# Experts 1 to 3 of a fused attention and expert kernel: word conversion dealt out 3, 1, 2, 2, weight splits begun one place sooner, two tiles for converted words

## The chip, the core and the metric

One core of a Trainium2 chip runs the whole program. The metric is the device time in microseconds of one execution; the time given for a kernel is the median of its runs. The engines are TensorE (PE in the rows; its weight loads PEld), VectorE (DVE), ScalarE (ACT), GpSimd (POOL) and SyncE (SP), which issues nearly all transfers from one in-order queue (SPq).

## The reference

Three layers follow one another: a gated linear recurrence over 768 positions, four experts mixed by normalised probabilities, and a feed-forward layer with h − tanh(h).

```python
# recurrence, for each of 4 x 8 heads of width 48
state = alpha[:, :, t, :, None] * state + np.einsum('bhd,bhe->bhde', k[:, :, t], v[:, :, t])
y[:, :, t] = np.einsum('bhd,bhde->bhe', q[:, :, t], state)
# four experts on x of 3072 x 384, w1[e] 384 x 1024, w2[e] 1024 x 384
for e in range(E):
    h = np.maximum(x @ w1[e], 0.0)
    out += p[:, e:e + 1] * (h @ w2[e])
# last layer, w_in 384 x 2048, w_out 2048 x 384, given in float64
h = x @ w_in
g = h - np.tanh(h)
return (g @ w_out).astype(np.float32)
```

The weights of the last layer are float64, so the chip gets them as 64-bit words and turns them into float32 itself.

## The kernel before

The program has three stages. In the first (about 0 to 332 us) the recurrence runs in chunks, woven into expert 0. In the second (about 332 to 921 us) experts 1, 2 and 3 run on all 3072 tokens. In the third (921 us to the end) the last layer runs. Every float32 product is made from three passes in a faster format: each operand is split into a high part (a cast on ScalarE, `hi`) and a low part (a subtraction on GpSimd, `lo`), and the product is high·high + low·high + high·low.

The change lies in the second stage and in the last block of expert 0 before it. The second stage is 36 **steps**, numbered 0 to 35 here: for each expert g = 1, 2, 3, three pairs of token blocks (p = 0, 1, 2, each block 512 tokens), and for each pair four pairs of feature tiles (fp = 0 to 3). A step is one call of `pair_stage`. It computes four 128x512 tiles of x @ w1 by a scheme that shares sums and differences of weights (`ws`, made by `w_pair`) and of tokens (`tb`, `ta`, made by `forms`), so that eleven products of three matmuls do the work of twelve. Each of the four results ends in one VectorE sum, in this order: L713 (`pc`), L727 (`u`), L736 (`pa`), L743 (`u2`). After each sum come the ReLU on ScalarE (`hh`, L596) and the low part on VectorE (`hl`, L597), and then the generator yields; I call the point after it a **place**, 0 to 3. After a place, `mm2` runs nine matmuls with w2 for a tile that was finished three places earlier.

At each place the caller also issues pieces of side work:

- `conv_all` (generator `bits`) converts the last layer's weights, in 32 pieces of 128x384 words. A piece takes six VectorE instructions, its **words**: L49, L52, L55, L58, L61, L65. Its result is then split by a ScalarE cast (L478) and a GpSimd subtraction (L479) into the tile `wo`, and SyncE stores `wo` to DRAM (`w64s`). There is one `wo` tile, so the cast for one piece waits for the store of the piece before.
- `w_pair` splits two weight tiles, in four pieces, one at each place: first `hi(wa)` on ScalarE with four short sums on GpSimd (L447 to L450, for `ws`); then `lo(wa)` and `hi(wb)`; then `lo(wb)` and `hi(ws)`; then `lo(ws)` and the loads of the next two raw weight tiles (`wraw`, two buffers).
- `forms` prepares the token sums in steps 1, 2, 5 and 6.

The Tile framework puts the semaphores in, and each engine runs its instructions in the order of the program. PSUM holds two tiles for the four results (`pa`, `pc`), so a product that reuses one of them waits for the sum that reads it: the last product of a step, made with s4 of `ws`, waits for L736.

Of the kernel before, what the change touches and what calls it, by code (L numbers as in the profile page):

```python
# [10 lines left out]
F32R = mybir.dt.float32r  # L11
# [30 lines left out]
def words_to_f32(nc, pool, raw, res):  # L42

    n = raw.shape[1]
    r2 = raw.bitcast(I32).rearrange("p (n two) -> p n two", two=2)
    lo, hi = r2[:, :, 0], r2[:, :, 1]
    t1 = pool.tile([P, n], I32, name="t1", tag="t1")
    t3 = pool.tile([P, n], I32, name="t3", tag="t3")
    nc.vector.tensor_scalar(out=t1, in0=hi, scalar1=3, scalar2=0x7FFFFFFF,  # L49
                            op0=ALU.logical_shift_left, op1=ALU.bitwise_and)  # L50
    yield
    nc.vector.scalar_tensor_tensor(out=t1, in0=hi, scalar=-2147483648, in1=t1,  # L52
                                   op0=ALU.bitwise_and, op1=ALU.bitwise_or)
    yield
    nc.vector.tensor_scalar(out=t3, in0=lo, scalar1=29, scalar2=0x40000000,  # L55
                            op0=ALU.logical_shift_right, op1=ALU.bitwise_or)
    yield
    nc.vector.tensor_tensor(out=t3, in0=t1, in1=t3, op=ALU.bitwise_xor)  # L58
    yield
    t5 = pool.tile([P, n], I32, name="t5", tag="t5")  # L60
    nc.vector.tensor_scalar(out=t5, in0=hi, scalar1=1, scalar2=21,  # L61
                            op0=ALU.logical_shift_left, op1=ALU.logical_shift_right)
    yield
    wf = pool.tile([P, n], F32, name="wf", tag="wf", bufs=2)
    nc.vector.scalar_tensor_tensor(out=wf, in0=t5, scalar=897.0, in1=f32(t3), op0=ALU.is_ge, op1=ALU.mult)  # L65
    res.append(wf)
# [117 lines left out]
def tile_kernel(ctx: ExitStack, tc: tile.TileContext, qka, a0, v, vT, pT, w12, w64, out):  # L184
# [281 lines left out]
    def conv_all(pool):  # L466

        raws, wfs, outs = [], [], []

        def load(i, half):  # L470
            raw = pool.tile([P, 384], I64, name="r64", tag="r64", bufs=2)
            nc.sync.dma_start(out=raw, in_=w64[i, :, half])
            raws.append(raw)

        def store(i, half):
            wf = wfs.pop(0)
            o = pool.tile([P, 2, 384], F32R, name="wo", tag="wo")
            nc.scalar.copy(o[:, 0], wf)  # L478
            nc.gpsimd.tensor_tensor(out=o[:, 1], in0=wf, in1=f32(o[:, 0]), op=ALU.subtract)  # L479
            outs.append((i, half, o))  # L480

        load(*conv[0])
        load(*conv[1])
        yield
        for k, (i, half) in enumerate(conv):
            for j, _ in enumerate(words_to_f32(nc, pool, raws.pop(0), wfs)):
                yield
                if j == 1 and k:
                    store(*conv[k - 1])
                    if k + 1 < len(conv):  # L490
                        load(*conv[k + 1])
                if j == 4 and outs:
                    i_, h_, o = outs.pop()
                    nc.sync.dma_start(out=w64s[i_][:, :, h_], in_=f32(o))
            yield
        store(*conv[-1])
        yield
        i_, h_, o = outs.pop()
        nc.sync.dma_start(out=w64s[i_][:, :, h_], in_=f32(o))
# [251 lines left out]
    with tc.manual_schedule():  # L751
# [106 lines left out]
        for si, st in enumerate(steps0):  # L858
            g, bi, t0, n, f, last = st
            bl = blocks0  # L860
            if f == 0:
                nxt = (g, *bl[bi + 1]) if not last else None
                if last:
                    early.close()
                    late["p"] = main.enter_context(tc.tile_pool(name="psx", bufs=1, space=PSUM))
                    late["w"] = main.enter_context(tc.tile_pool(name="wx", bufs=1))
                    acc.extend(late["w"].tile([P, KB, 512], F32, name=f"acc{i}", tag=f"acc{i}") for i in (4, 5))
                    late["s"] = mid.enter_context(tc.tile_pool(name="pairs", bufs=1))
                    late["c"] = mid.enter_context(tc.tile_pool(name="conv", bufs=1))
                    side = [forms(0, h, form_load(0, h)) for h in range(2)]  # L870

                if not last:
                    first, goal = done[0], ready((bl[bi + 1][0] + bl[bi + 1][1]) // C - 1) + LEAD
                    loaded = split = False
                    share = [first + (goal - first) * k // 16 for k in range(17)]
            ph = mm1(st)
            evac1(st, ph)
            pend.append(st)
            if not last:
                points(min(goal, share[2 * f + 1]))  # L880
            flush({5: 2, 6: 3, 7: 3}.get(f, 1) if last else 1)
            if not last:
                points(min(goal, share[2 * f + 2]))
                if not loaded and done[0] >= goal - LEAD:
                    loaded = True
                    x_load(*nxt)
                    p_load(*nxt)
                if not split and done[0] >= goal - LEAD + 3:
                    split = True
                    for kb in range(KB):  # L890
                        x_parts(*nxt[1:], kb)
                if bi == 0 and f < 4:
                    w_prep(4 + f)
                if bi == 0 and f == 4:
                    w_load(8)
                    w_load(9)
                    p_norm()
                    p_load(0, 0, 256)
            else:

                if f == 1:
                    pair_tile(0)
                    pair_tile(1)
                if f == 2:
                    for j in range(KB):
                        pair_load(0, j, 0)
                if f in (2, 6):
                    side.append(w_pair(8 + f // 4 * 2))
                if 1 <= f < 5:
                    for _ in range(2):  # L910
                        next(side[(f - 1) // 2], None)
                for t in side[2:]:
                    next(t, None)
                if f == 6:
                    for j in (0, 2, 1):
                        pair_load(1, j, 0)
                if f == 2:
                    fl = late["w"].tile([112, NU], F32, name="fl", tag="fl")
                    nc.vector.tensor_scalar(out=fl, in0=flags, scalar1=2.0 ** 60, scalar2=None, op0=ALU.is_le)
                    rs = late["w"].tile([112, 1], F32, name="rs", tag="rs")  # L920
                    nc.vector.tensor_reduce(out=rs, in_=fl, axis=mybir.AxisListType.X, op=ALU.add)
                if f == 3:
                    pc = rolling(0)[0:1, 0:1]
                    nc.tensor.matmul(pc, rs, ones, start=True, stop=True)
                    ci = const.tile([1, 1], I32, name="ci", tag="ci")
                    nc.vector.tensor_copy(ci, pc)
                if f == 5:
                    ok_count = nc.values_load(ci, min_val=0, max_val=112 * NU)
            if f == 3:
                x_keep(t0, n)  # L930
# [8 lines left out]
        for k, (g, p, fp) in enumerate(group):  # L939
            if k in (0, 4):  # L940
                raw = [form_load(k // 4 + 1, h) for h in range(2)]
            if k in (1, 2, 5, 6):
                side.append(forms(k // 4 + 1, k % 4 - 1, raw.pop(0)))

            if p == 2 and fp > 1:
                j = (g + 1) * 8 + 2 * fp - 4
            elif p == 0 and fp in (1, 2):
                j = g * 8 + 2 + 2 * fp
            else:
                j = None  # L950
            if j is not None and j < 32:
                side.append(w_pair(j))
            for pos in pair_stage(g, p, fp, fp == 3 and k + 1 < len(group)):
                po_out()
                if k > 2:
                    for _ in range(2 if fp and not (k in (5, 6) and pos < 2) else int(pos == 1)):
                        next(bits, None)
                for t in side:
                    next(t, None)
                if k == len(group) - 1 and pos >= 1:  # L960
                    x_split(4, 0, pos - 1)
            if fp == 1:
                for n in range(2):
                    p_load(g, (2 * p + n) * 512, 512)
            if j is not None and j >= 32:
                w_prep(j)
                w_prep(j + 1)
# [87 lines left out]
```

## Time and profile before

| | |
|---|---|
| median of 3 runs | 1334.12 us (1333.34 to 1334.77) |
| the profiled execution's own time | 1332.25 us |
| its span, first to last instruction | 1330.4 us |
| TensorE busy | 1287.2 us, 97% |
| VectorE busy | 896.9 us, 67% |
| ScalarE busy | 609.4 us, 46% |
| GpSimd busy | 536.0 us, 40% |
| mean granted TensorE clock | 0.989 |

Busy times of TensorE are made from pipelined matmuls whose ends are modelled, so 97% is not a share of its peak. What can be won without fewer matmuls is the time in which TensorE waits. The profiled execution is 1.87 us below the median of the runs.

### The profile page before, as it was taken

To read this page: it belongs to the slowest core of one execution; us is meant where nothing else is said; L and a number is where in the kernel's file an instruction comes from. 1 tells how busy PE (TensorE), PEld (TensorE's weight loads), DVE (VectorE), ACT (ScalarE), POOL (GpSimd) and SP (SyncE) were. 2 spreads that over 40 slices of the span, in tenths; PEclk is the share of its full clock that TensorE was granted. 3 is DMA by queue.
4 is the path that set the end of the run, shared out by engine and by line. 5 is a ranking of instruction groups with operands and counts; after the bars stand their busy time and mean duration, and the time that the engine had idled before them with its cause. 6 is when DMAs were issued, how large, how long until landed. Compare 5 with 4: busy or idle time off the path is not lost.

```text
span 1330.4 us, 18547 instructions
## 1 busy us (share of the span) xinstructions
PE 1287.2 (97%) x6747; PEld 1049.9 (79%) x6748; DVE 896.9 (67%) x1383; ACT 609.4 (46%) x1096; POOL 536.0 (40%) x487
## 2 busy tenths in 40 slices
PE   6799999999999999999999999999999999999997
PEld 4688888887878787778887788888888888888885
DVE  7678667624456657766666666665878787878785
ACT  3334333323433334333333333334777777777764
POOL 4211011004433134532044522114777676767664
PEclk8899999999999999999999999999999999999999
DMA  8365544416462725462616251517200000000000
GB/s 269 100 179 149 155 138 122 146 50 216 164 233 92 247 71 202 128 210 82 213 56 245 86 190 64 202 52 293 98 22 3 24 2 25 0 25 0 24 1 27
DMA packets 86389, 153.24 MB, mean 115 GB/s; under 512 B 7568, under 2 KB 43664, under 8 KB 86032
## 3 DMA queue, kind: packets, MB, share of 16 engines
q1 hardware_dynamic: 76304, 147.24, 33.1%
q10 hardware_dynamic: 9984, 4.72, 1.4%
q8 instruction: 55, 0.90, 0.3%
q14 instruction: 46, 0.38, 0.1%
HBM read 115.71 MB, written 36.23 MB: 114 GB/s over the span
## 4 chain that ended last, share of the span: by engine, by line
PE 83%; DVE 6%; DMA 3%; issue 3%; ACT 2%; POOL 2%; SPq 0%; POOLq 0%; DVEq 0%; ACTq 0%
PE po L641 39%; PE ph L589 21%; PE ph L674 18%; PE pa L308 2%; DMA w64s<-wo 2%; PE pa L341 1%; PE pa L344 1%; DVE hl L597 1%; ACT hh L596 1%; DMA wraw<-w 1%; POOL tb L547 1%; DVE fg L260 1%; PE ph L779 1%; PE pa L303 1%; PE pa L333 1%
## 5 line engine op out<-in xcount | busy, mean ns | idle before, releaser
L641 PE MATMUL po<-hh,w 128*128 128x512 f32 (+1 forms) x1776 | 451.1, 389 | 0.0
L641 PEld LDWEIGHTS po<-hh,w 128*128 128x128 f32 x1776 | 327.4, 189 | 74.0 <-issue 3.5
L589 PE MATMUL ph<-xt,w 128*128 128x512 f32 (+1 forms) x1368 | 326.7, 385 | 0.3 <-DVE ptmp L663 0.3
L589 PEld LDWEIGHTS ph<-xt,w 128*128 128x128 f32 x1368 | 251.8, 192 | 52.5 <-issue 1.2
L641 PE MATMUL po<-hl,w 128*128 128x512 f32 (+1 forms) x888 | 247.7, 387 | 1.2 <-DVE hl L621 1.2
L674 PE MATMUL ph<-xt,w 128*128 128x512 f32 x864 | 234.2, 392 | 1.7 <-DVE hl L597 0.9
L641 PEld LDWEIGHTS po<-hl,w 128*128 128x128 f32 x888 | 165.8, 190 | 35.9 <-DVE hl L621 1.6
L674 PEld LDWEIGHTS ph<-xt,w 128*128 128x128 f32 x864 | 162.3, 188 | 38.2 <-DVE hl L597 1.3
L596 ACT ACTIVATE hh<-ph 128x512 fp32r<-128x512 f32 (+1 forms) x128 | 73.1, 571 | 244.3 <-PE ph L589 145.0
L597 DVE SCALAR_TENSOR_TENSOR hl<-ph,hh 128x512 fp32r<-128x512 f32 (+1 forms) x128 | 84.1, 657 | 143.5 <-ACT hh L596 143.4
L75 POOL TENSOR_SCALAR gmk<-gu 128x512 int32<-128x512 f32 x96 | 143.1, 1491 | 49.0 <-ACT gu L71 48.3
L621 POOL TENSOR_TENSOR hl<-gg,hh 128x512 fp32r<-128x512 f32 x94 | 121.8, 1296 | 54.1 <-ACT hh L619 54.1
L479 POOL TENSOR_TENSOR wo<-wf,wo 128x384 fp32r<-128x384 f32 x32 | 35.1, 1098 | 235.4 <-ACT wo L478 235.4
L702 ACT COPY ut<-ph 128x512 f32<-128x512 f32 x108 | 63.3, 586 | 115.3 <-PE ph L674 115.3
L674 PE MATMUL ph<-xt,ws 128*128 128x512 f32 x324 | 106.6, 399 | 9.7 <-DVE ph L736 5.6
L71 ACT ACTIVATE gu<-ph 128x512 f32<-128x512 f32 x96 | 57.6, 600 | 114.7 <-PE ph L589 68.7
L667 POOL TENSOR_TENSOR acc<-acc,ptmp 128x512 f32<-128x512 f32 x51 | 65.0, 1295 | 102.3 <-DVE ptmp L663 102.3
L76 DVE SCALAR_TENSOR_TENSOR ghu<-ph,gu 128x512 f32<-128x512 f32 x96 | 66.3, 691 | 51.8 <-ACT gt L72 51.5
L674 PEld LDWEIGHTS ph<-xt,ws 128*128 128x128 f32 x324 | 60.8, 189 | 28.2 <-DVE ph L736 8.6
L80 DVE COPY_PREDICATED gg<-gmk,ph 128x512 f32<-128x512 int32 x96 | 72.0, 750 | 10.1 <-POOL gmk L75 0.3
L365 POOL TENSOR_TENSOR state<-state,fc 112x192 f32<-112x192 f32 x20 | 10.1, 506 | 169.9 <-DVE state L356 145.4
L79 DVE SCALAR_TENSOR_TENSOR gg<-gs,ghu 128x512 f32<-128x512 f32 x96 | 66.4, 692 | 14.9 <-DVE ghu L78 2.9
(121 smaller groups left out, 1512.3 us busy)
## 6 DMA issues: line engine op xcount, KB each, us to landing
xt<-xs SPq DMA_DIRECT2D x54, 512.0 KB, 5.8
xt<-xb SPq DMA_DIRECT2D x27, 512.0 KB, 5.7
r<-w SPq DMA_DIRECT2D x32, 384.0 KB, 5.0
w64s<-wo SPq DMA_DIRECT2D x32, 384.0 KB, 3.0
w<-w64s SPq DMA_DIRECT2D x16, 768.0 KB, 7.4
qk<-qka SPq DMA_DIRECT2D x24, 448.0 KB, 6.8
wraw<-w SPq DMA_DIRECT2D x26, 384.0 KB, 5.2
pb<-pn SPq DMA_DIRECT2D x23, 256.0 KB, 4.6
```

The costliest lines, as they stand in the source:

```text
L75: nc.gpsimd.tensor_scalar(out=mk, in0=u, scalar1=T2, scalar2=None, op0=ALU.is_gt)
L76: nc.vector.scalar_tensor_tensor(out=hu, in0=ph, scalar=C4, in1=u, op0=ALU.mult, op1=ALU.mult)
L79: nc.vector.scalar_tensor_tensor(out=gg, in0=s2, scalar=B2, in1=hu, op0=ALU.add, op1=ALU.mult)
L80: nc.vector.copy_predicated(out=gg, mask=mk, data=ph)
L589: nc.tensor.matmul(ph[:, :n], w[:, a, 0, kb * P:(kb + 1) * P], x[:, b, kb, :n], start=m == 0, stop=m == len(seq) - 1)
L596: nc.scalar.activation(a[:, :n], ph[:, :n], AF.Relu)
L597: nc.vector.scalar_tensor_tensor(out=b[:, :n], in0=ph[:, :n], scalar=0.0, in1=f32(a[:, :n]), op0=ALU.max, op1=ALU.subtract)
L621: eng.tensor_tensor(out=b, in0=gg, in1=f32(a), op=ALU.subtract)
L641: nc.tensor.matmul(po[d, pool][:, :n], w[:, wi, 1, d * P:(d + 1) * P], r[:, :n], start=first and pi == 0, stop=last_ and pi == 2)
L667: nc.gpsimd.tensor_tensor(out=a_, in0=a_, in1=tmp, op=ALU.add)
L674: nc.tensor.matmul(ph, w[:, a], x[:, b], start=start and m == 0, stop=m == len(seq) - 1, skip_group_check=not start)
L702: nc.scalar.copy(t, ph)
```

## The change

Four edits, all about when side work is issued:

1. At steps with fp > 0 (from step 3 on, but for steps 5 and 6) the words are dealt out 3, 1, 2, 2 over the four places, where they were dealt out 2, 2, 2, 2.
2. The weight pairs that are needed at p = 0, fp = 2 and 3 (weights 12, 14, 20, 22, 28, 30) are begun at place 3 of the step two before their use, where they were begun at place 0 of the step just before it. The pairs begun at p = 2 stay where they were. In the last block of expert 0, the pair 8 is begun at f = 1 in place of f = 2.
3. `wo` has two tiles.
4. To pay for it, the temporary `t5` of a word conversion uses the buffer of `t1`.

```diff
-    t5 = pool.tile([P, n], I32, name="t5", tag="t5")
+    t5 = pool.tile([P, n], I32, name="t5", tag="t1")
...
-            o = pool.tile([P, 2, 384], F32R, name="wo", tag="wo")
+            o = pool.tile([P, 2, 384], F32R, name="wo", tag="wo", bufs=2)
...
-                if f in (2, 6):
+                if f in (1, 6):
                     side.append(w_pair(8 + f // 4 * 2))
...
             if p == 2 and fp > 1:
                 j = (g + 1) * 8 + 2 * fp - 4
-            elif p == 0 and fp in (1, 2):
-                j = g * 8 + 2 + 2 * fp
+            elif p == 0 and fp < 2:
+                j = g * 8 + 4 + 2 * fp
             else:
                 j = None
-            if j is not None and j < 32:
-                side.append(w_pair(j))
             for pos in pair_stage(g, p, fp, fp == 3 and k + 1 < len(group)):
                 po_out()
+                if j is not None and j < 32 and pos == (0 if p else 3):
+                    side.append(w_pair(j))
                 if k > 2:
-                    for _ in range(2 if fp and not (k in (5, 6) and pos < 2) else int(pos == 1)):
+
+                    for _ in range((3, 1, 2, 2)[pos] if fp and not (k in (5, 6) and pos < 2) else int(pos == 1)):
                         next(bits, None)
                 for t in side:
                     next(t, None)
```

How rows move is shown at two places. The first is VectorE in step 25 (g = 3, p = 0, fp = 1), from the first sum to the third; `t` and `r` are temporaries and raw words of the conversion. Before:

```order
L713 TENSOR_TENSOR ph<-ut,ph 128x512
L597 SCALAR_TENSOR_TENSOR hl<-ph,hh 128x512
L55 TENSOR_SCALAR t_6623<-r_6563 128x384
L58 TENSOR_TENSOR t_6623<-t_6622,t_6623 128x384
L727 TENSOR_TENSOR ut<-ut,ph 128x512
L597 SCALAR_TENSOR_TENSOR hl<-ut,hh 128x512
L61 TENSOR_SCALAR t_6827<-r_6563 128x384
L65 SCALAR_TENSOR_TENSOR wf<-t_6827,t_6623 128x384
L736 TENSOR_TENSOR ph<-ut,ph 128x512
```

and in the change:

```order
L713 TENSOR_TENSOR ph<-ut,ph 128x512
L597 SCALAR_TENSOR_TENSOR hl<-ph,hh 128x512
L55 TENSOR_SCALAR t_6623<-r_6563 128x384
L58 TENSOR_TENSOR t_6623<-t_6622,t_6623 128x384
L61 TENSOR_SCALAR t_6801<-r_6563 128x384
L727 TENSOR_TENSOR ut<-ut,ph 128x512
L597 SCALAR_TENSOR_TENSOR hl<-ut,hh 128x512
L65 SCALAR_TENSOR_TENSOR wf<-t_6801,t_6623 128x384
L736 TENSOR_TENSOR ph<-ut,ph 128x512
```

One word, L61, has gone from between L727 and L736 to ahead of L727.

The second is ScalarE from the end of step 24 (the ReLU of its `u`) to the third copy of step 25; L440 is `hi`, L478 the cast into `wo`. Before:

```order
L596 ACTIVATE hh<-u_6660 128x512
L702 COPY ut<-ph 128x512
L596 ACTIVATE hh<-ph 128x512
L702 COPY u_6783<-ph 128x512
L478 CAST wo<-wf 128x384
L440 CAST w<-wraw 128x768
L702 COPY ut<-ph 128x512
L596 ACTIVATE hh<-ut 128x512
L440 CAST w<-wraw 128x768
L702 COPY ut<-ph 128x512
```

and in the change:

```order
L596 ACTIVATE hh<-u_6660 128x512
L440 CAST w<-wraw 128x768
L702 COPY ut<-ph 128x512
L596 ACTIVATE hh<-ph 128x512
L702 COPY u_6792<-ph 128x512
L478 CAST wo<-wf 128x384
L440 CAST w<-wraw 128x768
L702 COPY ut<-ph 128x512
L596 ACTIVATE hh<-ut 128x512
L440 CAST ws<-sf 128x384
```

The first split of the pair, `hi(wa)`, now stands ahead of the first copy of the step, and the whole pair is one place ahead; on GpSimd the `lo` parts move with it.

## Rows read from the trace of the kernel before

**Rows 1.** Busy time by stretch: PE, PEld, DVE, ACT, POOL; granted clock; DMA.

```profile
460.00:480.00 20.00, 17.69 (x69) 13.76 (x68) 9.58 (x17) 5.11 (x9) 5.68 (x5) 0.91 0.46 177
...
950.00:1330.40 380.40, 371.98 (x1612) 302.37 (x1610) 296.91 (x447) 263.72 (x473) 263.32 (x192) 1.00 0.04 13
```

**Rows 2.** What TensorE waited for, 322 to 921 us: total, times, longest.

```profile
PE ph L674 <- DVE ph L736: 5.6, 7, 1.3
PE ph L674 <- ACT ut L702: 2.4, 2, 1.9
PE ph L674 <- POOL ws L443: 1.6, 4, 1.1
PE ph L674 <- DVE hl L597: 0.9, 1, 0.9
PE ph L674 <- DVE u L743: 0.4, 1, 0.4
PE ph L674 <- DMA xt<-xs: 0.4, 1, 0.4
```

**Rows 3.** Line 713, the first sum of each step: min/median/max ns, first and last start.

```profile
L713 DVE TENSOR_TENSOR ph<-ut,ph x36: 682/696/698, 333.9 to 903.1; 128x512 f32<-128x512 f32 x36
```

**Rows 4.** Timeline of step 0, an undisturbed one: start, duration, what, [idle before].

```profile
338.76 0.69 DVE L727 TENSOR_TENSOR ut<-ut,ph 128x512 f32<-128x512 f32 x1 [2.81 <-PE ph L674]
...
342.18 0.70 DVE L736 TENSOR_TENSOR ph<-ut,ph 128x512 f32<-128x512 f32 x1 [1.34 <-PE ph L674]
...
343.96 0.40 PE L674 MATMUL ph<-xt,ws 128*128 128x512 f32 x1
...
348.33 0.59 ACT L702 COPY ut<-ph 128x512 f32<-128x512 f32 x1 [1.42 <-PE ph L674]
...
349.71 0.70 DVE L713 TENSOR_TENSOR ph<-ut,ph 128x512 f32<-128x512 f32 x1 [1.48 <-PE ph L674]
```

**Rows 5.** Timeline at the end of step 7 and in step 23: store and cast of wo.

```profile
456.68 0.77 SPq L494 DMA_DIRECT2D w64s<-wo  x1
...
465.12 0.51 ACT L478 CAST wo<-wf 128x384 fp32r<-128x384 f32 x1 [4.24 <-DMA w64s<-wo]
...
466.17 0.96 PE L674 MATMUL ph<-xt,ws 128*128 128x512 f32 x3 [1.92 <-ACT ut L702]
...
720.20 0.50 PE L674 MATMUL ph<-xt,ws 128*128 128x512 f32 x1 [0.30 <-DVE ph L736]
```

**Rows 6.** What ScalarE waited for, 332 to 915 us.

```profile
ACT wo L478 <- DMA w64s<-wo: 11.1, 4, 4.2
```

**Rows 7.** Timeline of step 25, places 0 and 1.

```profile
748.22 4.11 POOL L443 TENSOR_TENSOR w<-wraw,w 128x768 fp32r<-128x768 f32 x2
...
748.82 1.81 DVE L597 SCALAR_TENSOR_TENSOR hl<-ut,hh 128x512 fp32r<-128x512 f32 x1 [0.70 <-ACT hh L596]
...
750.55 1.99 DVE L61 TENSOR_SCALAR t<-r 128x384 int32<-128x384 int32 x1
...
753.05 0.69 DVE L736 TENSOR_TENSOR ph<-ut,ph 128x512 f32<-128x512 f32 x1
...
753.79 0.50 PE L674 MATMUL ph<-xt,ws 128*128 128x512 f32 x1 [1.00 <-DVE ph L736]
```

**Rows 8.** Timeline of step 7: two words while GpSimd is idle.

```profile
461.51 0.55 DVE L52 SCALAR_TENSOR_TENSOR t<-r,t 128x384 int32<-128x384 int32 x1
461.98 0.35 DVE L55 TENSOR_SCALAR t<-r 128x384 int32<-128x384 int32 x1
```

**Rows 9.** Timeline of step 3: TensorE waits for the split of ws.

```profile
383.49 0.99 POOL L443 TENSOR_TENSOR ws<-sf,ws 128x384 fp32r<-128x384 f32 x1
...
384.54 0.73 PE L674 MATMUL ph<-xt,ws 128*128 128x512 f32 x2 [1.05 <-POOL ws L443]
```

**Rows 10.** Timeline of step 2: load of raw weights, and the split that waits for it.

```profile
365.43 1.68 SPq L412 DMA_DIRECT2D wraw<-w  x2
...
370.67 0.84 ACT L440 CAST w<-wraw 128x768 fp32r<-128x768 f32 x1 [3.36 <-DMA wraw<-w]
```

## The prediction

> **What bounds the kernel now.** I read the busy time by stretch first, then what TensorE waited for, then the steps of the second stage one by one in the timeline. After 950 us TensorE is busy 371.98 of 380.40 us, and nothing there is touched by the change [rows 1], so what the second stage wins or loses should reach the end one to one. The question is how much that stage wastes. Line 713 runs once in each of the 36 steps, first at 333.9 and last at 903.1 us [rows 3]: 569.2 us for 35 steps. An undisturbed step, from 333.9 to 349.71 [rows 3, 4], takes 15.81 us, so 35 of them need 553.3, and **15.9 us are lost**. That is the ceiling of this change, apart from what lies at the stage's two ends.
>
> The waits of TensorE say where it is lost [rows 2]: 5.6 us in 7 waits for the sum L736, 2.4 in 2 for a ScalarE copy, 1.6 in 4 for the split weights `ws`, 0.4 for L743, 0.4 for a transfer of tokens, and 0.9 for a low part at 332 us, before the first L713. Without the last that is 10.4 us in 15 waits. Around the longest wait the granted clock averages 0.91 over 20 us [rows 1], full rate being 2.4 GHz and the lower level 1.2, which costs 20 x 0.09 = 1.8 us. The remaining 15.9 − 10.4 − 1.8 = 3.7 us over 15 waits make 0.24 us for each wait on top of its listed idle time (the end of a matmul is modelled late and the first one after a pause is slower). I price a wait at its idle time plus 0.24.
>
> **The change part by part.**
>
> *Two tiles for `wo`.* At the end of step 7 ScalarE stands 4.24 us before the cast L478, because the only `wo` tile is still being stored: the store was issued at 456.68, among the loads of the next tokens, and the cast began at 465.12. The copy behind it is late, and TensorE stands 1.92 us [rows 5]. ScalarE had four such waits, 11.1 us [rows 6]. They explain both copy waits, 2.4 + 2 x 0.24 = 2.9; the clock, 1.8, since the lower level appears only where TensorE had just stood for that long; and in step 23 one wait for L736, 0.30 + 0.24, with the wait for L743 that follows it, 0.4 + 0.24 [rows 2, 5]. With two tiles a cast needs the store of two pieces before, which was issued about six words, so at least three places, earlier. This part wins 2.9 + 1.8 + 0.5 + 0.6 = **5.8 us**.
>
> *Splits one place sooner.* In step 3 the low part of `ws` starts at 383.49 and TensorE waits 1.05 us for it [rows 9]; all four waits of this kind are in steps whose pair began at p = 0, and their sum is 1.6. A place is a quarter of a step, 3.95 us, more than the longest of them, so they go: 1.6 + 4 x 0.24 = **2.6 us**. The split needs its raw weights: in step 2 their load was issued at 365.43, and ScalarE waited 3.36 us until 370.67 [rows 10]. Load and split both move one place forward. On SyncE's queue the loads of weights 14 and 15 now stand ahead of the stores of `forms`, and the first raw tile comes free after the previous pair's `lo(wa)`, two places before the load stands in the program, so I expect no such wait. The pair 8, moved in the last block of expert 0, is worth nothing: ScalarE and GpSimd have room there, the next loads still stand behind the store of the second form, and the 0.9 us for a low part at 332 us stays.
>
> *Words 3, 1, 2, 2.* In step 0 VectorE had 2.81 us of room ahead of L727 but only 1.34 ahead of L736, and TensorE's product at 343.96 began 1.08 us after L736 ended at 342.88 [rows 4]. So the words at place 1 may take 1.34 + 1.08 = 2.4 us before TensorE feels it. A word alone takes 0.35 to 0.55 us [rows 8]; two fit easily. But in step 25 L61 took 1.99 us and the low part before it 1.81, both while two `lo` splits ran on GpSimd for 4.11 us, and TensorE waited 1.00 us for L736 [rows 7]. The VectorE instructions with only SBUF operands seem to be held until the GpSimd instruction beside them ends; the sums, which read PSUM, take 0.69 to 0.70 us even there [rows 4, 7].
>
> The Trainium skill, in "SBUF — State Buffer", section "SBUF: two separate sides", says the same as a rule: VectorE and GpSimd share a port pair under an exclusive lock, held for the whole instruction, and the other fully blocks. The trace agrees (1.99 us against 0.35 alone). By that rule alone the change would give a smaller gain, because it also puts `lo` splits beside the three words of place 0; that is the second rival below.
>
> The other six waits for L736 sum to 5.3 us and fall in steps 2, 10, 11, 13, 14 and 25, all steps in which a pair is split (1.34, 0.59, 1.06, 0.58, 0.76 and 1.00 of the 5.6 in rows 2). In steps 2, 14 and 25 the two `lo` move a place forward, and place 1 keeps at most the short `lo(ws)`. For step 25 I place them at about 746.0 to 750.1. Then the three words end near 748.3, L727's low part near 750.4, the one word left at place 1 by 751.7 at worst, and L736 must begin by 751.9 (the product would run at 752.6). So these three go: 3.1 + 3 x 0.24 = **3.8 us**. In steps 10 and 11 the split stays where it was, and in step 13 a `wo` on GpSimd still holds `lo(wb)` back to place 1; one word fewer saves one of two blocked instructions. Between nothing and all of 2.2 + 0.7 = 2.9 I take half, **1.5 us**.
>
> *`t5` in `t1`'s buffer.* It adds a wait of L61 for L58, both on VectorE and already in this order. Independent words overlap a little (L55 starts 0.47 us after L52, which takes 0.55 [rows 8]), so the 32 pieces can each lose about 0.1 us in VectorE's room. I put nothing on the path; the low end is nothing, the high end 32 x 0.1 = 3.2 us if no room were left.
>
> **The sum.** 5.8 + 2.6 + 3.8 + 1.5 = 13.7 us. Against it I set one new wait of about the mean size, 0.9 us, for places where three words now stand beside a split. That leaves 12.8 us: the profiled execution's 1332.25 becomes 1319.4, and since it lay 1.9 below the median, the median 1334.1 becomes **1321.3**.
>
> **Rivals.**
>
> *Only the plain waits go.* The words' waits stay in sum, since splits and words both moved and may meet elsewhere. Then the gain is 5.8 + 2.6 = 8.4 us, 1325.7. For it: GpSimd's queue is in order, and a `wo` that waits for ScalarE can hold a `lo` back to the old place. Against: place 1 has one word fewer everywhere.
>
> *Place 0 becomes the jam.* In steps 13, 14, 25 and 26 three words can each wait out a `lo` of 4.11 / 2 = 2.05 us: with their own time some 7.1 us. Place 0 has 2.81 of room, and L727 then has about 1.8 us before TensorE needs its buffer (twelve matmuls of 0.23 us after the result, less 0.27 and 0.69), so 2.5 us are lost in each, 10 in all: 13.7 − 10 = 3.7 us of gain, 1330.4. For it: rows 7. Against: a held word runs between two `lo`, and by my placement step 25 has about 1 us to spare at L727.
>
> *The change does nothing that counts.* The waits go to the next late thing, such as the ScalarE copies: 1334.1, within 2.7 us. Against: VectorE, ScalarE and GpSimd all have idle time in an undisturbed step [rows 4].
>
> *Slower: the raw weights hold ScalarE at place 3.* `hi(wa)` now stands ahead of the step's first copy, which had 1.42 us of idle time before it [rows 4] and some 0.5 us more before TensorE needs it. If a load were issued only when ScalarE is already there, each of six pairs would wait a whole landing, 370.67 − 365.43 = 5.2 us, plus 0.84 for the cast, less 1.9: 4.1 us each, 24.7 in all, and 1334.1 + 24.7 − 12.8 = 1346. It decides from a wait of 3.7 us for each pair on. Against: the load follows a `lo(wa)` two places earlier.
>
> **How the numbers follow.** The forecast (a gain of 10 to 15) has a chance of 0.61, only the plain waits 0.17, the jam 0.11, no effect 0.06, slower 0.05. A measurement of this kernel can tell about 0.2%, 2.7 us, from no change: faster 0.89, same 0.06, slower 0.05. Alone, the forecast's range is 1319 to 1324: its low end is all 15.9 gone but the transfer wait (0.4 + 0.24), its high end half of the words' 5.3 us missing. The range that should hold 8 in 10 reaches from 1318.5 over the first rival to 1328.5, where part of the jam begins.
>
> **What would show it.** Right: ScalarE's waits for the `wo` store near nothing, no TensorE wait for `ws`, the granted clock at 1.00 from 460 to 480, waits for L736 below 2.5 us in sum, and the first to last L713 in 556 to 559 us. The words are the doubtful step: TensorE waiting for L727, or for a copy behind a `hi` that waited for its load, would show the jam or the slower rival. The prediction would be wrong if the stage shortens and the last one does not start earlier by as much.

## The result and the profile after

The changed kernel takes 1320.04 us (median of 6 runs, 1317.72 to 1320.72) against 1333.73 us (6 runs, 1330.83 to 1336.48) for the kernel before beside it: ratio 0.9897, 95% interval 0.9881 to 0.9914, or 13.7 us less. The forecast was 12.8 us less. The profiled execution took 1320.48 us with a span of 1318.7 us.

The waits of TensorE over the second stage, after (total, times, longest), answer to [rows 2]:

```profile
PE ph L674 <- DVE ph L736: 1.2, 2, 0.6
PE ph L674 <- DVE hl L597: 0.9, 1, 0.9
PE ph L674 <- DMA xt<-xs: 0.4, 1, 0.4
PE ph L589 <- DVE ptmp L663: 0.3, 1, 0.3
```

The waits for the ScalarE copy, for `ws` and for L743 are gone, and of seven waits for L736 two are left. The one for L597 lies ahead of the first L713, as before. The one on line 589 comes at 909.0 us, behind the last L713, in the first matmuls of the last layer; the kernel before has the same 0.33 us wait at 921.2, just outside the window of [rows 2]. Line 713 after, as in [rows 3]:

```profile
L713 DVE TENSOR_TENSOR ph<-ut,ph x36: 681/697/698, 335.5 to 891.0; 128x512 f32<-128x512 f32 x36
```

The stretch from the first to the last L713 is 555.4 us, 13.8 shorter than before. After it come 1318.7 − 891.0 = 427.7 us, against 1330.4 − 903.1 = 427.3 before, so the rest of the program hands the gain on to the end. The busy time by stretch (columns as in [rows 1]):

```profile
460.00:480.00 20.00, 19.59 (x86) 15.76 (x85) 12.78 (x19) 6.15 (x11) 8.33 (x7) 1.00 0.37 139
```

TensorE is busy 19.59 of the 20 us in which it had been busy 17.69 at a lower clock. Around the end of step 7 (timeline; answers to [rows 5]) the cast no longer stands before the store:

```profile
458.99 0.50 ACT L478 CAST wo<-wf 128x384 fp32r<-128x384 f32 x1
...
461.05 1.43 PE L674 MATMUL ph<-xt,w 128*128 128x512 f32 x5 [0.41 <-DMA xt<-xs]
```

ScalarE has no wait for a store of `wo` in the whole stage [rows 6]. Its first split of weights 14 and 15, which had stood 3.36 us in step 2 for raw weights [rows 10], comes a place sooner, at the end of step 1, and finds them there: the last load before it is issued at 355.92, ahead of the stores of `forms` on SyncE's queue, 8.9 us before the split.

```profile
355.92 0.33 SPq L412 DMA_DIRECT2D wraw<-w  x1
...
364.83 0.84 ACT L440 CAST w<-wraw 128x768 fp32r<-128x768 f32 x1
```

Step 25 in the timeline (answers to [rows 7]; its first sum is the first row):

```profile
732.97 0.70 DVE L713 TENSOR_TENSOR ph<-ut,ph 128x512 f32<-128x512 f32 x1 [1.09 <-PE ph L674]
...
735.55 1.25 DVE L58 TENSOR_TENSOR t<-t,t 128x384 int32<-128x384 int32 x1
...
736.35 4.09 POOL L443 TENSOR_TENSOR w<-wraw,w 128x768 fp32r<-128x768 f32 x2
...
736.84 1.89 DVE L61 TENSOR_SCALAR t<-r 128x384 int32<-128x384 int32 x1
...
738.65 0.67 DVE L727 TENSOR_TENSOR ut<-ut,ph 128x512 f32<-128x512 f32 x1
...
742.20 0.68 DVE L736 TENSOR_TENSOR ph<-ut,ph 128x512 f32<-128x512 f32 x1
...
743.01 0.43 PE L674 MATMUL ph<-xt,ws 128*128 128x512 f32 x1
```

L61 is held nearly as long as before (1.89 us for 1.99), but now ahead of L727, and TensorE does not have to wait: the product at 743.01 carries no bracket. VectorE is busy no less in all (906.7 us, 9.8 more), so the held words have moved to where there is room; they have not become shorter.

One of the two waits that are left, in step 10:

```profile
499.82 4.10 POOL L443 TENSOR_TENSOR w<-wraw,w 128x768 fp32r<-128x768 f32 x2
...
500.42 1.81 DVE L597 SCALAR_TENSOR_TENSOR hl<-ut,hh 128x512 fp32r<-128x512 f32 x1 [0.70 <-ACT hh L596]
...
502.15 2.19 DVE L58 TENSOR_TENSOR t<-t,t 128x384 int32<-128x384 int32 x1
504.26 0.68 DVE L736 TENSOR_TENSOR ph<-ut,ph 128x512 f32<-128x512 f32 x1
...
505.00 0.50 PE L674 MATMUL ph<-xt,ws 128*128 128x512 f32 x1 [0.61 <-DVE ph L736]
```

Place 1 has one word (L58) instead of two, but the low part ahead of it is now held as well. In the kernel before it ran free, ahead of two held words:

```profile
505.94 0.69 DVE L597 SCALAR_TENSOR_TENSOR hl<-ut,hh 128x512 fp32r<-128x512 f32 x1 [0.70 <-ACT hh L596]
```

There GpSimd's subtraction for `wo` stood ahead of the two `lo`, which began 2.91 us after the start of L727 (507.46 and 504.55). With three words at place 0 a piece is finished sooner, its `wo` moves ahead with it, and the two `lo` begin 0.79 us after L727 (499.82 and 499.03). So L736 comes as late as before (0.59 us of wait then, 0.61 now). With the words 3, 1, 2, 2 alone step 10 shows the same low part of 1.81 us and the same wait of 0.61.

### The profile page after: what moved, and what is told of

Read it like the earlier page. It is cut to its first block, busy times and chain, and to the rows that moved or that the text cites. A ratio compares the mean times of both kernels' runs of the same rounds, so it can differ in the third digit from the quotient of the medians.

```text
span 1318.7 us, 18568 instructions
## 1 busy us (share of the span) xinstructions
PE 1285.5 (97%) x6748; PEld 1051.6 (80%) x6748; DVE 906.7 (69%) x1383; ACT 610.0 (46%) x1096; POOL 536.8 (41%) x487
## 4 chain that ended last, share of the span: by engine, by line
PE 88%; DVE 4%; issue 2%; DMA 2%; ACT 1%; POOL 1%; SPq 0%; DVEq 0%; POOLq 0%; ACTq 0%
PE po L641 42%; PE ph L674 20%; PE ph L589 20%; PE pa L308 2%; PE pa L341 1%; PE pa L344 1%; DVE fg L260 1%; DMA xt<-xs 1%; PE pa L303 1%; DMA xraw<-xr 1%; PE pa L333 1%; DVE hl L597 0%; DVE prod L280 0%; DMA wraw<-w 0%; DVE fg L270 0%
## 5 line engine op out<-in xcount | busy, mean ns | idle before, releaser
L597 DVE SCALAR_TENSOR_TENSOR hl<-ph,hh 128x512 fp32r<-128x512 f32 (+1 forms) x128 | 84.1, 657 | 143.8 <-ACT hh L596 143.7
```

The source lines that it names most:

```text
L597: nc.vector.scalar_tensor_tensor(out=b[:, :n], in0=ph[:, :n], scalar=0.0, in1=f32(a[:, :n]), op0=ALU.max, op1=ALU.subtract)
```

## The experiments

A step's loss is the distance from its L713 to the next, less 15.795 us, the median of these distances in the kernel before. Nearly all that is lost falls into three groups of steps which hardly touch one another (step 6 loses 0.3 us in every kernel and is in none): **A**, steps 7, 8, 22 to 24, 31 and 32 (`wo` stores); **B**, steps 2, 3, 14, 15 and 25 to 27 (splits begun at p = 0); **C**, steps 10 to 13 (words beside the splits begun at p = 2). The table gives each group's loss in us, from the starts of L713 in the timelines. Ratios are to the kernel before, run beside each (there it took 1333.7 to 1335.1 us), with 95% intervals; where none stands there was one run. Stretch and groups come from the one profiled execution of each kernel.

| kernel | time us | ratio | stretch us | A | B | C |
|---|---|---|---|---|---|---|
| before | 1333.73 | | 569.2 | 6.3 | 6.7 | 3.1 |
| the change | 1320.04 | 0.9897 (0.9881 to 0.9914) | 555.4 | 0.5 | 0.0 | 1.8 |
| two `wo` tiles alone | 1329.43 | 0.9961 (0.9945 to 0.9977) | 564.5 | 1.2 | 7.0 | 3.1 |
| splits sooner alone | 1326.62 | 0.9946 (0.9931 to 0.9961) | 561.6 | 5.1 | 0.8 | 3.1 |
| words 3, 1, 2, 2 alone | 1333.22 | 0.9983 (0.9972 to 0.9994) | 566.0 | 5.0 | 6.1 | 1.8 |
| change, one `wo` tile | 1325.8 | | 561.2 | 6.3 | 0.0 | 1.8 |
| change, splits as before | 1326.6 | | 561.6 | 0.3 | 6.2 | 1.8 |
| change, words 2, 2, 2, 2 | 1324.53 | | 557.6 | 1.1 | 0.4 | 3.0 |
| before, zero fills as `lo` | 1328.47 | | 561.2 | 4.9 | 3.6 | 0.0 |
| before, `t5` in `t1` | 1335.89 | | 568.5 | 5.3 | 7.2 | 3.1 |
| change, words 4, 0, 2, 2 | 1322.54 | 0.9901 (0.988 to 0.9922) | 557.0 | 1.3 | 2.5 | 0.0 |
| change, all splits sooner | 1319.46 | 0.9887 (0.987 to 0.9903) | 554.7 | 0.9 | 0.0 | 0.0 |
| change, steps 10 and 11 sooner | 1320.05 | 0.9892 (0.9875 to 0.9909) | 554.0 | 0.9 | 0.1 | 0.0 |

### One part alone

Two tiles for `wo`, with `t5` in `t1` to make the space:

```diff
-    t5 = pool.tile([P, n], I32, name="t5", tag="t5")
+    t5 = pool.tile([P, n], I32, name="t5", tag="t1")
...
-            o = pool.tile([P, 2, 384], F32R, name="wo", tag="wo")
+            o = pool.tile([P, 2, 384], F32R, name="wo", tag="wo", bufs=2)
```

> The kernel before with two wo tiles (and t5 in t1's buffer) alone. My theory prices this part at 5.8 us, independent of the others: the first-to-last L713 stretch goes from 569.2 to about 563.4 us, the time to about 1328; ScalarE's waits for the store vanish, the waits of TensorE for L736 in steps 2, 10, 11, 13, 14 and 25 (5.3 us) and for ws (1.6 us) stay. Rival: the store wait only hides the next late thing, and the stretch shortens by less than 3 us.

Waits of TensorE:

```profile
PE ph L674 <- DVE ph L736: 6.0, 7, 1.3
PE ph L674 <- POOL ws L443: 1.8, 4, 1.1
```

The copy waits and the wait for L743 are gone, and only they: 4.7 us of the stretch, where 5.8 were expected. Group A gives 5.1 of them, and 0.2 is lost again in step 14, as it is with `t5` in `t1` alone. There are still seven waits for L736. The one in step 23 [rows 5] stays, for another reason; here is that step in this kernel's timeline:

```profile
714.49 1.12 POOL L479 TENSOR_TENSOR wo<-wf,wo 128x384 fp32r<-128x384 f32 x1 [3.50 <-ACT wo L478]
714.65 1.37 DVE L52 SCALAR_TENSOR_TENSOR t<-r,t 128x384 int32<-128x384 int32 x1
715.57 4.05 POOL L443 TENSOR_TENSOR w<-wraw,w 128x768 fp32r<-128x768 f32 x2
715.94 2.00 DVE L55 TENSOR_SCALAR t<-r 128x384 int32<-128x384 int32 x1
717.86 0.68 DVE L736 TENSOR_TENSOR ph<-ut,ph 128x512 f32<-128x512 f32 x1
...
718.60 0.50 PE L674 MATMUL ph<-xt,ws 128*128 128x512 f32 x1 [0.58 <-DVE ph L736]
```

The copy is in time now, and two words at place 1, each held beside GpSimd, make the same sum late. Step 23 needed two edits, the `wo` tile and the words: without either it keeps a wait for L736 (0.58 us in the change with words 2, 2, 2, 2, and 0.75 in the change with one `wo` tile).

The splits one place sooner, the pair 8 at f = 1 with them (the split hunks of the diff alone):

```diff
-            elif p == 0 and fp in (1, 2):
-                j = g * 8 + 2 + 2 * fp
+            elif p == 0 and fp < 2:
+                j = g * 8 + 4 + 2 * fp
...
+                if j is not None and j < 32 and pos == (0 if p else 3):
+                    side.append(w_pair(j))
```

> The kernel before with only the splits begun one place sooner. My theory: the four waits for ws go (2.6 us), and the wait for L736 in step 2, where no words run, goes (1.6 us); in steps 13, 14 and 25 two words still stand at place 1, now mostly beside lo(ws), so about half of their 2.9 + 0.2 us goes: stretch near 563.5 us, gain 5 to 6.5. Rival: the splits only move the jam to place 0, and the stretch shortens by 2.6 us or less, or TensorE waits for L727 or for a ScalarE copy.

```profile
PE ph L674 <- DVE ph L736: 2.5, 4, 1.1
PE ph L674 <- ACT ut L702: 2.2, 2, 1.9
```

No wait for `ws` is left, and of L736's 5.6 us the 3.1 of steps 2, 14 and 25 are gone, with the words still at 2, 2, 2, 2. The expectation left half of the waits in steps 14 and 25; they went whole, and group B gave 5.9 us. The stretch is 7.6 us shorter, more than the 5 to 6.5 expected, but 1.2 of that is in group A, where the clock did not fall in this execution (below).

The words alone:

```diff
-                    for _ in range(2 if fp and not (k in (5, 6) and pos < 2) else int(pos == 1)):
+                    for _ in range((3, 1, 2, 2)[pos] if fp and not (k in (5, 6) and pos < 2) else int(pos == 1)):
```

> The kernel before with only the words dealt out 3, 1, 2, 2. My theory: one held word less at place 1 in steps 10, 11, 13, 14 and 25, so about half of their 4.0 + 1.2 us goes, and nothing else: gain 2 to 3 us, stretch near 566.5. Rival (VectorE was simply too full at place 1, whatever GpSimd does): all of it goes, gain 5 us, stretch near 564. Other rival (the words matter only together with the sooner splits): gain under 1 us.

Group C falls from 3.1 to 1.8 us and group B by 0.6; the time moves by 0.17%, hardly more than can be told. Of the stretch's 3.2 us less, 1.3 is in group A, where the clock did not fall in this execution (below).

### The change without one part

Each is the changed kernel with that part of the diff put back (one `wo` tile and `t5` in a buffer of its own; the pairs begun as before; words 2, 2, 2, 2).

> The changed kernel with one wo tile again (and t5 in its own buffer): sooner splits and words 3, 1, 2, 2 stay. My theory: the copy waits of steps 7 and 31 and the late L736 and L743 of step 23 come back, so the first-to-last L713 stretch goes from 555.4 to about 559 us, or 560.5 if the lower clock comes with the wait in step 7, as it did in the kernel before but in neither of the runs that kept that wait. Rival (the parts only work together): much of the gain goes, stretch above 563.

> The changed kernel with the weight pairs begun where they were before: two wo tiles and words 3, 1, 2, 2 stay. My theory: the waits for ws come back (steps 1, 2, 14, 25), the wait of step 2 for L736, and one held word each in steps 14 and 25: stretch near 562 us. Rival (the words alone free place 1): stretch near 558, only the waits for ws.

> The changed kernel with the words dealt out 2, 2, 2, 2 again. My theory: the second held word comes back in steps 11, 13 and 25 (0.45, 0.9 and 0.3 us), nothing else: stretch near 557 us. Rival (the words carry the gain at L736): all six waits for L736 come back, stretch near 561.

The stretches, 561.2, 561.6 and 557.6 us, lie near the expectations (560.5 with the lower clock, 562 and 557) and away from their rivals (above 563, near 558, near 561). Taken from the change, `wo` is worth 561.2 − 555.4 = 5.8 us (some 1.5 of them by the clock, which fell in that execution), the splits 6.1, the words 2.2: 14.1 in sum, against 13.8 for all three. The table shows that the same groups come back as were there before, so the three parts add up; only step 23 is shared.

These kernels also show what the clock has to do with it. The six profiled kernels with one `wo` tile all have the same ScalarE copy wait of 1.9 to 2.0 us at the end of step 7. Here are the 20 us around it and the first matmuls after it, with the splits alone:

```profile
460.00:480.00 20.00, 17.19 (x74) 13.51 (x73) 11.03 (x17) 5.21 (x10) 7.35 (x6) 1.00 0.37 143
```

```profile
465.07 0.96 PE L674 MATMUL ph<-xt,ws 128*128 128x512 f32 x3 [1.93 <-ACT ut L702]
465.87 1.55 PE L641 MATMUL po<-hh,w 128*128 128x512 f32 x6
```

and in the change with one `wo` tile:

```profile
460.00:480.00 20.00, 17.77 (x71) 13.95 (x70) 10.34 (x16) 5.22 (x9) 7.36 (x6) 0.91 0.35 134
```

```profile
463.96 1.65 PE L674 MATMUL ph<-xt,ws 128*128 128x512 f32 x3 [1.94 <-ACT ut L702]
465.41 2.20 PE L641 MATMUL po<-hh,w 128*128 128x512 f32 x6
```

The same nine matmuls take (1.65 − 0.96) + (2.20 − 1.55) = 1.3 us longer there. The granted clock fell (0.91) before, in this last one and with the zero fills, and did not (1.00) with the splits alone, the words alone and `t5` in `t1`. Less the transfer wait that step 7 has besides, steps 7 and 8 lose 3.5 to 3.9 us in the first three and 2.2 in the others. So the fall of the clock is worth about 1.5 us, and the 2.2 that is left is the copy wait at the price of the prediction, 1.92 + 0.24. The clock did not fall in this stage in any of the seven profiled kernels with two `wo` tiles. Each of these kernels was profiled once, so whether one and the same kernel sometimes shows the fall and sometimes not isn't shown; the length of the pause does not decide it.

### What holds the words

In `w_pair` of the kernel before, each subtraction `lo` is replaced by three zero fills of the same tile on GpSimd, so the low parts of these weights are left out. They keep GpSimd busy for longer, if anything (4.7 to 4.8 us for two `lo`, which took 4.1), and read nothing (later lines have a number one higher).

```diff
-            nc.gpsimd.tensor_tensor(out=o[:, 1], in0=t, in1=f32(o[:, 0]), op=ALU.subtract)
+            for _ in range(3):
+                nc.gpsimd.memset(f32(o[:, 1]), 0.0)
```

> The kernel before, with each lo subtraction of w_pair replaced by three GpSimd fills of the same tile with zero; the low parts of these weights are left out. A fill of 768 elements should take about 0.8 us (the fill of 384 took 0.42), three of them about as long as one lo (2 us), but they read nothing. If VectorE's words are held because GpSimd reads through what they read through, the words with two SBUF inputs (L52, L58, L65) and the low part of u run free beside the fills (0.55 and 0.69 us) and most of the 5.3 us of waits for L736 go. If GpSimd being busy is enough, all words are still held for the length of a fill, and the waits shrink only as far as three short holds are shorter than one long one. If GpSimd has nothing to do with it and VectorE is too full at place 1, all waits for L736 stay.

Waits of TensorE, and two places of the timeline with words beside the fills:

```profile
PE ph L675 <- DVE ph L737: 0.4, 1, 0.4
```

```profile
510.21 4.80 POOL L444 MEMSET w<- 128x768 f32 x6
511.19 0.56 DVE L58 TENSOR_TENSOR t<-t,t 128x384 int32<-128x384 int32 x1
...
523.89 4.70 POOL L444 MEMSET w<- 128x768 f32 x6
...
524.50 0.69 DVE L598 SCALAR_TENSOR_TENSOR hl<-ut,hh 128x512 fp32r<-128x512 f32 x1 [0.70 <-ACT hh L597]
525.11 0.53 DVE L61 TENSOR_SCALAR t<-r 128x384 int32<-128x384 int32 x1
525.74 0.56 DVE L65 SCALAR_TENSOR_TENSOR wf<-t,t 128x384 f32<-128x384 int32 x1
```

With GpSimd just as busy, L58 takes 0.56 us (2.19 in step 10 of the change), the low part 0.69 (1.81), and the waits for L736 fall from 5.6 us to 0.4. It is so throughout: the seven L58 and seven L65 that start beside a fill take 0.55 to 0.56 us, where the seven L58 that start beside a split in the kernel before take 1.25 to 2.20. A hold for the length of one fill (about 0.8 us) would show in these times, so it is not the shorter GpSimd instruction that frees them. What costs is neither that GpSimd is busy nor the number of words, but words beside a subtraction, which reads SBUF where the fill does not. Group B keeps 3.6 us here, because waits for `ws` stay (1.8 us in three). The Trainium skill ("SBUF — State Buffer", section "SBUF: two separate sides") says that a VectorE instruction with two SBUF inputs contends for the lock only with a GpSimd instruction that reads SBUF. L58, L65 and the low part agree. L61, with one input, takes 0.53 us here against 0.35 for L55 of the same form on a quiet GpSimd [rows 8].

### The shared temporary

`t5` in `t1`'s buffer, in the kernel before. (The second `wo` tile takes the space of this buffer, so the price is taken here.)

> The kernel before with only t5 in t1's buffer. I priced it at nothing on the path, at most 0.1 us in VectorE for each of 32 pieces: stretch 569.2 us, or 567.5 where the lower clock of step 8 stays away. Rival: the added wait of L61 delays sums where VectorE has no room (steps 11, 14, 25), up to 1 us more.

The stretch is 568.5 us and the granted clock 1.00 from 460 to 480 us, so it is 1.0 us above the 567.5 expected for that clock. Group C is that of before, and B is 0.5 us longer (7.2, where two `wo` tiles with the same `t5` show 7.0); in both kernels step 14 loses 0.24 more. Another 0.4 is a longer transfer wait in step 7 (0.80 us for 0.39), which the transfers also show without `t5` (0.88 with the splits alone). So `t5` was not quite free in the kernel before, where the prediction put nothing: about 0.5 us in this execution, which leans to the expectation's rival and is far from the upper bound of 3.2.

### How far place 0 carries

```diff
-                    for _ in range((3, 1, 2, 2)[pos] if fp ...
+                    for _ in range((4, 0, 2, 2)[pos] if fp ...
```

> The changed kernel with the words dealt out 4, 0, 2, 2. If what is left at L736 (1.2 us in steps 10 and 11) is one held word at place 1, it goes: stretch near 553.7 us, 1.7 below the changed kernel. The jam of place 0, which I put as a rival of the prediction, is tested here: four words there, each held by up to 2.05 us, would make L727 late in steps 13, 14, 25 and 26, TensorE would wait for L727 or for the copy behind it, and the stretch would be above 556.

No wait for L736 is left and group C is 0.0, but two waits for L727 are new. The first, in step 14:

```profile
PE ph L674 <- DVE ut L727: 1.9, 2, 1.0
```

```profile
562.67 2.09 DVE L58 TENSOR_TENSOR t<-t,t 128x384 int32<-128x384 int32 x1
564.79 1.89 DVE L61 TENSOR_SCALAR t<-r 128x384 int32<-128x384 int32 x1
...
566.60 0.67 DVE L727 TENSOR_TENSOR ut<-ut,ph 128x512 f32<-128x512 f32 x1
...
567.33 0.98 PE L674 MATMUL ph<-xt,w 128*128 128x512 f32 x3 [0.83 <-DVE ut L727]
```

The rival's jam exists; it begins with the fourth word.

### The splits of steps 10 and 11

First every pair begun at p = 2 one place sooner too (its use one step later is unchanged):

```diff
-            if p == 2 and fp > 1:
-                j = (g + 1) * 8 + 2 * fp - 4
+            if p == 2 and fp in (1, 2):
+                j = (g + 1) * 8 + 2 * fp - 2
...
-                if j is not None and j < 32 and pos == (0 if p else 3):
+                if j is not None and j < 32 and pos == 3:
...
```

(The lines left out keep the last layer's weight loads in their old steps.)

> The changed kernel with the pairs of p = 2 (steps 10, 11, 22, 23) begun one place sooner as well, at place 3 of the step before. If the lo splits beside place 1 are what is left of the waits for L736 (1.2 us in steps 10 and 11), these go: stretch near 554 us, time 1.5 us below the changed kernel's. Rival: the three words of place 0 now stand beside the lo splits in these steps and TensorE waits for L727 or for a copy instead: stretch 555 or more.

Group C goes to 0.0, but step 22 loses 1.4 us (0.4 in the change), of which step 23 makes up 0.5, and step 0 loses 0.7, where TensorE waits 0.4 us for a transfer of tokens. The timeline at the sum that ends step 22, the first of step 23:

```profile
698.47 2.16 POOL L443 TENSOR_TENSOR w<-wraw,w 128x768 fp32r<-128x768 f32 x1
698.96 1.89 DVE L61 TENSOR_SCALAR t<-r 128x384 int32<-128x384 int32 x1
...
700.77 0.68 DVE L713 TENSOR_TENSOR ph<-ut,ph 128x512 f32<-128x512 f32 x1
...
701.98 0.58 ACT L702 COPY u<-ph 128x512 f32<-128x512 f32 x1
...
702.61 0.73 PE L674 MATMUL ph<-xt,ws 128*128 128x512 f32 x2 [0.59 <-ACT u L702]
```

There a held word makes L713 late, and with it the copy behind the ReLU that reads this sum. So the last kernel begins only the two pairs of the first of these experts sooner and leaves those of the second:

```diff
+            if g == 1 and p == 2:
+                j = 14 + 2 * fp if fp in (1, 2) else None
...
-                if j is not None and j < 32 and pos == (0 if p else 3):
+                if j is not None and j < 32 and pos == (0 if p and g > 1 else 3):
```

> The change, with the two pairs begun at p = 2 of the first of the three experts also begun one place sooner (steps 10 and 11), and those of the second (steps 22 and 23) left where they were. Theory (a wait for L736 comes from a low split that lies beside places 0 and 1, and goes with it): steps 10 and 11 lose their 0.85 and 1.47 us as they did where all pairs were begun sooner, and step 22 keeps its 0.4, since there the sooner pair had put a held word ahead of L713. Stretch of L713 553.7 us (553.2 to 554.5), 1.7 below the change, time 1318.3. Rival (what the sooner pairs of steps 10 and 11 win turns up elsewhere, as it did in steps 0 and 22): stretch 555 to 556, time 1320. The difference is too small for the times to settle; the stretch and the waits of TensorE decide.

```profile
PE ph L674 <- DVE hl L597: 0.9, 1, 0.9
PE ph L674 <- DMA xt<-xs: 0.9, 1, 0.9
```

Between the first and the last L713 TensorE waits only for the transfer, and the stretch, 554.0 us, is the shortest of all. It lies inside the theory's 553.2 to 554.5 and below the rival's 555: 1.8 us are won in group C, 0.4 given back in step 7, where the transfer wait goes from nothing to 1.3 us between the executions of these kernels. The times (0.9892 against 0.9897) don't separate it from the change.

## Why the prediction was right

The mechanism was right, and the sum came within 1 us: 13.8 us on the stretch, 13.7 in the median, for 12.8. Luck has a share in how near it came: about 1.5 us of the stretch's 13.8 is a fall of the clock in the profiled execution of the kernel before, and without it some 12.3 would have come back (an estimate, 13.8 − 1.5). How many of the other runs had that fall isn't on record. The 0.9 deducted for a new wait did not come, so the parts before it, 13.7, were nearer than the sum.

- **What bounds it.** 15.9 us were said to be lost in the stretch, and 13.8 came back. The first L713 moved from 333.9 to 335.5 us, but among kernels with and without the earlier pair 8 it lies anywhere from 333.9 to 338.2, so that is not the change's; it is also why the two profiled spans differ by only 11.7. It goes with the granted clock of the first 100 us: 0.88 in the kernel before, 0.83 in the change, and 0.81 with the zero fills, where the first L713 comes at 338.2.
- **Two `wo` tiles, 5.8.** Group A lost 6.3 us and now 0.5. The pieces came near too: steps 7 and 8 won 3.7 (forecast 1.9 + 0.24 for the wait and 1.8 for the clock, which is rather 1.5), steps 22 to 24 1.3 (forecast 1.2), steps 31 and 32 0.8 (forecast 0.7). But 1.5 of it is there only where the clock falls, and of the 0.5 for L736 in step 23 the store was one cause of two. The prediction's reason for the clock, that it fell where TensorE had just stood so long, is not enough: three kernels with the same pause kept 1.00.
- **Splits, 2.6 + 3.8 = 6.4.** Group B went from 6.7 to 0.0; alone they win 5.9 there. The two `lo` of step 25 lie 3.4 to 7.5 us after its first sum (736.35 and 740.44, less 732.97), the same as the forecast's placement (746.0 and 750.1, less the 742.60 at which L713 started there before). In the stage no load made ScalarE late, so the slower rival had no ground. The one wait for raw weights that is left, 2.9 us at the end of expert 0, is the same in both kernels, and so is TensorE's 0.9 us behind it; there the earlier pair 8 was worth nothing, as forecast.
- **Words, half of 2.9 = 1.5.** Group C lost 3.1 and now 1.8: 1.3. It was not a half everywhere: step 13 lost its whole wait, step 11 part, step 10 nothing, since its low part is held in the word's place. The half was a guess between nothing and all, and that it came near is luck.
- **The new wait, 0.9.** This is the term that was mis-sized: no wait is new in the change, and 13.7 before this deduction is what came. Three words beside a subtraction, as in step 25, end in time; that place 0 would give way was right in kind and comes with four words, at 1.2 and 1.4 us in steps 14 and 25 in place of 2.5 in four steps.
- **`t5`, nothing.** About 0.5 us in the kernel before, and nothing in the change, where group B is 0.0.
- **What would show it.** Store waits, waits for `ws`, clock and L736 (1.2 us, below 2.5) came out as listed; the stretch ended 0.6 us below the 556 to 559 given, by the new wait that didn't come. That only the plain waits go was wrong, since group C and the waits for L736 in B fell too.

## What to carry to other kernels

Measure a step's pitch against an undisturbed one and sort the losing steps by cause: here three causes sat in three sets of steps, so their prices added up and each edit could be costed alone. When a short VectorE instruction takes four times its usual time, look at what GpSimd reads beside it, and move the one or the other to a place that ends in a sum with room. After taking away a wait, ask what is late next at the same instruction: in step 23 and step 10 a second cause stood right behind the first.

## What the hardware showed beyond that

- Around the same TensorE pause of 1.9 to 2.0 us, the granted clock averaged 0.91 from 460 to 480 us in three profiled kernels and 1.00 in three others; in the pair compared the nine matmuls behind it took 1.3 us longer. A single profile of each kernel can't tell whether such a drop belongs to the kernel.
- Zero fills on GpSimd (six in 4.7 us) left VectorE's two-input instructions at their quiet 0.56 and 0.69 us, where two subtractions in 4.1 us held them to 1.81 and 2.19.
